# A state-space convolution mixed with linear attention: turn scratch and normaliser scratch laid out anew, index cast on VectorE, and a new issue list with new engine and ring choices

## The chip, the cores and the metric

The kernel runs on one core of one Trainium2 chip. The metric is the device time of one execution in microseconds. Before the change the median of three runs is 265.28 us (264.55 to 266.64). The engines are TensorE (PE, matmuls; PEld, its weight loads), VectorE (DVE), ScalarE (ACT), GpSimd (POOL) and SyncE (SP), which only issues transfers. A transfer is split over 16 DMA engines. DVE and ACT share the casts that bring matmul results from PSUM to SBUF.

## The reference

The input u has 2048 positions of 512 channels. Two results are mixed by a gate g of each position:

```python
x = A_u
g = _sigmoid((x * gate_w).sum(-1, keepdims=True))
a = _A_ref(x, ...)      # S4 convolution
b = _B_ref(x, ...)      # linear attention, 32 heads of 16
return g * a + (1 - g) * b
```

The convolution's kernel is K[d, l] = Re(sum over n of C * exp(dt*A*l) * dt*B), with 128 complex states for each channel; y is the causal convolution of u with K (in the reference by a transform of length 4096), plus u times Dskip. The attention forms q, k, v from one weight, maps q and k by a small weight of each head, takes the softmax of the result and of its negative as 32 features, and divides phi_q (phi_k^T v) by phi_q (sum of phi_k) for each head. A last weight wo follows.

## The kernel before

**Order of the work.** The kernel first makes a list of 1058 steps (class Plan, L71 on). A step has an engine, the steps it depends on, and the buffers it takes and drops. Then it emits them in the order of a string: each pair of characters of ORDER is a step's number. Every engine runs its own steps in that order and waits at a step whose inputs aren't there; so a late step holds up all that stands behind it on its engine. Three more strings hold choices: SIDES says for each step that may run on either of two engines which one it is (mostly casts on ACT or DVE, some copies on DVE or GpSimd, the output issues on SP or ACT); RINGS says which of two PSUM rings a step takes (psP, two tiles, or the one that exists at that stage); WARM adds idle matmuls to chosen steps, and is all zeros.

**Stages.** (1) Up to about 24 us: loads, sine tables TB, TI, TJ from an index, transposes of u (xps, L504), weight folds (wtp, wps), polar tables. (2) About 24 to 72 us: keys and values (pk L709, vp L757, kn L774) on PE, with the forward transform of u (psAu L591, psBu L616), whose result goes through the scratch XUd in DRAM. (3) From about 72 us: the tables C and D, then, for 16 units of 32 channels, the convolution kernel: tables A (A1 L1100, A2 L1105, A3 L1110) and R (Rh L1117, Rl L1121) on DVE, the product kps (L183) on PE, the transform of K in two stages (psA L190, psB L196), the product with the spectrum of u (t, L1231, L1234, on DVE), the inverse transform psz (L1263), the turn, and psy (L1341, L1354), which adds the attention's part and is multiplied with the gate by DVE (ou, L1363, L1366, L1369). In between come four query blocks (pq L843, zs L863, em L913, ops L932, and for the last block bpsL L946). Channels come in blocks: three of 128 (Q = 0, 1, 2), then 64, 32 and 32.

**The turn.** Between psz and psy the data must change from (t, x) on partitions to (x, r). For every block but the last this goes through a DRAM scratch Zd. psz's result is cast to Zr (two buffers; L149 by P.copy), written (step zw, L1276) and read back in two halves (step zr, L1285) into ZT:

```python
F.Zd = g.dram.tile([32, 4, 32, nd], BF16, ...)                        # t x r d
nc.sync.dma_start(out=F.Zd[:, :, r0:r0 + ns, :].rearrange("t x r d -> (t x) r d"), in_=box.Z[:])   # L1276
nc.sync.dma_start(out=F.Z[64 * th:64 * th + 64], in_=F.Zd[:, 2 * th:2 * th + 2].rearrange("t x r d -> (x r) t d"))   # L1285
```

nd is the block's channels and ns = 1024/nd, so a written run is always 2 KB on each of 128 partitions and a read run is nd x 2 bytes (256 B for nd = 128), 32 of them on each partition. A block of 128 has four writes of 256 KB and two reads of 512 KB. The last block (32 channels) has no scratch: its psz (pszn, L1297) gives the turned form directly, cast to Z by two steps Zn.

**The normaliser.** A query block's 1/denominator (times 1 - g) is made on ACT and DVE (z1 to z5, among them L880 and L886), written by SP to a scratch apd (step aw, L899) and read back to all partitions (step ar, L906), two steps of two reads of 256 KB, into ax. DVE then multiplies the exponentials Eq with it (em, emL, L913). The scratch has 8 rows of 2 KB for each read, and each row goes to 16 partitions:

```python
in_=g.apd[b, i].rearrange("h m c -> h (m c)").unsqueeze(1).to_broadcast([8, 16, 1024])   # L906
```

**Index cast.** Step ifc (L238) casts eight columns of index values from int32 to f32 with nc.scalar.copy; the identity (L239) and the other index columns (L246 to L254) on DVE wait for it, and behind them the arguments of the sines (tg1, L269).

**Loads and outputs.** All loads are issued by SP: parameters (L216), wqk (L1502), small weights (L1497 to L1499), u in four groups (L1492). XUX is read from XUd (L1184, L1186) ahead of each t. Outputs (out, L1380; outL, L995) are issued by SP or ACT, two transfers a step; an output step of a block stands behind the last ou (or bsg) of it.

Of the kernel before, what the change touches and what calls it, by code (L numbers as in the profile page):

```python
# [11 lines left out]
ALU = mybir.AluOpType  # L12
# [58 lines left out]
class Plan:  # L71

    DIGITS = "0123456789abcdefghijklmnopqrstuvwxyzABCDEFGHIJKLMNOPQRSTUVWXYZ-_"
    ORDER = ("040B0H0K0d0y0C0D0L0s0I070J0M0P0g000S110j0N08010z0T0m0Q0e2R0a0p0q0r0_0W2T100U0O0V14120Y2U2x0A2S050k130Z2y2V2X2Z0R190v0t0u"
             "0b0c0w2_0l0E0X2W1516172L1a061b2Y022-30311y33340n030f0-"
             "0h1e1f0i1w2J18321c0F0o2B2K2M1n1z1H1g1A1o2D2C1d1p1I091x1E1J351Q1R2F1B0x1C2E0G2H1q36372G2I2P382N2Q391F3b2O3c4C1S3a4J4L4K4M"
             "3d3e4Q4R3f4U1Y3g4N1r4O1h4V3h1L4Y4-"
             "4P3i4Z4_3j4W4S53542z57504T3k4X1Z515b5d58521s1D593l5c3n5i5e55565j3m5a1G3o5q5f5g5s5r5t3p3r3q1T5m5n5u3s5v5h5o5k5w5x5B1P4D4E"
             "3w2v5l5p4F5y5F5C3y1U5H3x5G5I5J5z5A1V5D5E3t3z5U3D5K5V5M5N3A3R3E2w3F5W5L1O5_3G5O5Q5X5Y5Z3B3C1W605R5S1N3K3M1K3S1M5-"
             "5P3L634G642A615T653N673T6869626a666m6n6o3U6p3V3W3X3Y6b6c6q6d6r6s1t3Z3H3-1X3_3O1i1j41401_4221431-"  # L80
             "1k1l204445466e272923222b282d4748243P491m2a4a2c2e4b4g2f4c2g4d252h2o4e4h4i4n1u4j3u3v2j4p2i2l2k2m2q2p6i262s4q4o1v4k2n4u2r2t"
             "6f4v4w6j4r3I2u4x4y4z6g4l8l3J4A8p8m6t6u6k6v8q3Q4f4s6x6h8k8o6l8n8r8s6y6z6w6A6C4m4t4B8C6G8t6I6K8w8x8y8u6B6H6J4H8D8v6L6M6N7d"
             "8z8A8E4I8B7e7f8I7g8F6F9e8Q8G8H9b6O6P8R7h7j7i6Q6R8J9f7M7N8S6S6T6U6Vaeaf7O8W8X8K7k9g8L8T8U8Z8-"
             "938M8N7l6D8_7m8V7n6W6X6Y8O8P8Y7P94an7o7pao7q6_70717r90917Qa47S9295ag7R6Z7s6-"
             "72aha8a9966Ea7akaca5ai73aa75979998ajap7677a69aalatamab74ad7TaBaC7t797u7v7U78au7y7z7V7w7x9caq9naras7AavaH7W9d9h9o9paw7X9v"
             "aY9waK7Y7ZaDaL9q9raZ7a9x9y9zaIc57B7-aM9kc69D9EaQaEbX9L7Cb_aF7D9M7_9Ac07EaRaG9iaxaz80ay9B818285bYaA7Ga-"
             "7IaJ86879j9Fc19s7Jb-"
             "9l9m9Na_7bc7aNaOaPc3cbb2b37HbZc283aS9C7FaT849G9H9I9t89aUaWaV8baX7cccc8c99O9u9P9Q9R888cb87Kb9b0c4caceb19J8abacfcgbg8dck9K"
             "8ecl8f8gbbbh8hbcbibob4cP9Sbpbqcd9T8ichci7L8jcBcCcjcsdYcYctcucycDczdZd-cQcR9Ucmd_cHcvcw9W9Xcnbj9VbwbkblbxcocIbre0eLcp9Ze1"
             "e2b5b6eMbse3eUeVcxb7bye4cqbtbu9Ybdbe9-"  # L90
             "9_cAcrcSbme5cZdOdScEbfcFcGcTcUe6a0a1bve7dTdRdWeNa2e8cJcKe9bzbAedeecLeRcNcOa3eSeaebeOcMc_ePbBd0ecd1d7cVd8d9cWeCdfcXeWdPdU"
             "d2daefege-e_eQd3dbdQdgeTdVd4dndodXdhdcg1g2dieDeEdjeXbKfAbCbnbDbEbFeYfBeZf0f1bGc-dpbLddg7dqbHd5f2drbMf3f4f5bNfGbIbJbOezdk"
             "eAfDdsfEeBeIf6f7feffdldtbPdebQdBfCfHehdueifFejdmf8fgeJd6ekdvfIfJdyf9fafhfbg4fifKg5g6dwfjdzfkfcdxdCdEfLdAdFfMg3g8dGg9dHfN"
             "fleFelfdfmfpdDdLgagbgcgddIeGemeKfqeHfOfPfQfRgeenepfneofreqeresgfggghgifSfTfUfofsbRgjbSgkdJftetglfVfYfZgmgngobUbVgqfufWdM"
             "dNbWgpf-fvfxfygreufwevewexbTeydKfzfXf_g0gvgwgsgtgugx")
# [103 lines left out]
def prepare(P, nc, g, evict, psum):  # L199
# [11 lines left out]
    def S(name, fn, r="", w="", deps=()):  # L211
        return P.add("ACT", name, fn, deps, rw=(r, w))
# [59 lines left out]
    def sine(out, v, kv, w, turn=False):  # L272
        S("tgs", lambda: act(out=out(), in_=(low(v()) if not turn else low(v()).rearrange("p (h t) -> p t h", h=2)), func=ACT.Sin, scale=TURN), r="act " + kv, w=w)
# [1352 lines left out]
```

## Time and profile before

| what | value |
|---|---|
| median of 3 runs | 265.28 us |
| profiled execution, its own time | 266.07 us |
| span of the profile (first to last instruction) | 264.3 us |
| mean granted TensorE clock | 0.932 |
| DVE, ACT, PE busy | 232.5, 221.5, 207.2 us |
| DMA traffic | 35.93 MB, mean 136 GB/s |
| ACT table loads | 11, 1.28 us each |

In the profile a row of groups reads: line, engine, operation, output<-input, partitions x elements, count | busy time, mean ns of one | idle time before them and its releaser. A row of the timeline begins with start and duration; in brackets stand the idle time of the engine before the row and what ended it. A name with q (SPq, ACTq) is an issue by the queue and not work of the engine. A row of waits reads: who <- whom, total us, times, longest. A row of stretches has for each engine busy us and (x instructions), and the last two numbers are the mean busy share of the 16 DMA engines (it can exceed 1, since packets of one engine overlap) and GB/s. A row of the DMA queues reads: packets, MB, share of 16 engines.

### The profile page before, as it was taken

The numbers are of one execution on the slowest core, as the hardware profiler recorded it, in microseconds if no ns is written. First come the engines' busy times: TensorE is split into PE (matmuls) and PEld (weight loads), VectorE is DVE, ScalarE is ACT, GpSimd is POOL, SyncE is SP. The second block draws the span as 40 slices with busy tenths as digits, with TensorE's granted clock in tenths as the row PEclk, the third lists the DMA queues.
The fourth block names the chain that finished last, engine by engine and source line by source line (L and its number), as shares of the span: only waits on it lengthen the run. The fifth ranks groups of instructions, "written<-read, shape, count | busy, mean of one in ns | idle before, by whom it ended". The sixth has DMA issues, their size and how long they took to land.

```text
span 264.3 us, 10050 instructions
## 1 busy us (share of the span) xinstructions
PE 207.2 (78%) x4491; PEld 143.7 (54%) x4512; DVE 232.5 (88%) x315; ACT 221.5 (84%) x305; POOL 8.2 (3%) x21
## 2 busy tenths in 40 slices
PE   0766999999864879889776768999997598999750
PEld 0655655656633533456555247665775176965540
DVE  6699989889799999999999997999997998997630
ACT  6999998998899999899999898999998597755100
POOL 4700000000000000000000000000000000000000
PEclk9999999999976599999998688999999799999985
DMA  6995000454501892204160655159554589999775
GB/s 201 189 219 171 0 4 2 122 145 138 154 8 36 245 266 97 82 20 153 56 195 9 208 195 167 42 162 180 142 172 147 172 203 234 188 189 162 156 110 96
DMA packets 63323, 35.93 MB, mean 136 GB/s; under 512 B 40496, under 2 KB 57776, under 8 KB 63280
## 3 DMA queue, kind: packets, MB, share of 16 engines
q1 hardware_dynamic: 61424, 34.76, 53.2%
q8 instruction: 35, 0.57, 1.0%
q10 hardware_dynamic: 1856, 0.52, 1.0%
q14 instruction: 8, 0.07, 0.1%
HBM read 22.17 MB, written 13.11 MB: 133 GB/s over the span
## 4 chain that ended last, share of the span: by engine, by line
DVE 35%; PE 34%; DMA 8%; issue 7%; ACT 7%; SPq 6%; DVEq 0%; ACTq 0%
PE pk L709 5%; PE vp L757 4%; DVE Eq L913 3%; DVE A L1105 3%; DVE A L1100 3%; DMA ZT<-Zd 3%; DVE R L1117 3%; DVE R L1121 3%; SPq L1492 3%; DMA ax<-apd 2%; PE kps L183 2%; DVE E L1053 2%; PE psz L1263 2%; PE kvp L774 2%; DMA apd<-apm 2%
## 5 line engine op out<-in xcount | busy, mean ns | idle before, releaser
L68 ACT ACTIVATE cs<-args 128x1024 bf16<-128x1024 f32 x32 | 30.7, 1067 | 0.7 <-PE args L1023 0.7
L183 PEld LDWEIGHTS <-A 128*32 128x32 bf16 x1536 | 26.5, 160 | 6.1 <-issue 2.3
L183 PE MATMUL kps<-R,A 128*32 128x64 bf16 x1536 | 28.2, 229 | 1.9 <-DVE R L1121 1.2
L1263 PE MATMUL psz<-t,TI 128*128 128x512 bf16 x51 | 17.4, 446 | 5.0 <-DVE t L1231 3.2
L1100 DVE TENSOR_TENSOR A<-Ctab,Dtab 128x2048 bf16<-128x2048 bf16 x16 | 19.5, 1216 | 1.6 <-PE kps L183 1.6
L149 ACT CAST Zr<-psz 128x1024 bf16<-128x1024 f32 x15 | 15.2, 1021 | 5.8 <-PE psz L1263 4.3
L1121 DVE TENSOR_TENSOR R<-E,cs 128x2048 bf16<-128x2048 bf16 x16 | 19.4, 1215 | 0.1
L1105 DVE TENSOR_TENSOR A<-Ctab,Dtab 128x2048 bf16<-128x2048 bf16 x16 | 19.4, 1216 | 0.0
L1117 DVE TENSOR_TENSOR R<-E,cs 128x2048 bf16<-128x2048 bf16 x16 | 19.4, 1215 | 0.0
L68 ACT ACTIVATE Ek<-pk 128x512 bf16<-128x512 f32 x32 | 16.7, 599 | 1.9 <-PE pk L709 1.7
L68 ACT ACTIVATE Eq<-pq 128x512 bf16<-128x512 f32 (+1 forms) x28 | 16.6, 685 | 0.8 <-PE pq L843 0.7
L1231 DVE TENSOR_TENSOR t<-XUX,XK 128x2048 bf16<-128x2048 bf16 x14 | 16.7, 1216 | 0.4 <-ACT XK L149 0.4
L68 ACT ACTIVATE E<-args 128x1024 bf16<-128x1024 f32 x16 | 16.4, 1035 | 0.5 <-DVE R L1121 0.5
L757 PE MATMUL vp<-WW,xT 128*128 128x512 bf16 x59 | 16.2, 406 | 0.7 <-issue 0.6
L149 ACT CAST XA<-psA 128x1024 bf16<-128x1024 f32 (+1 forms) x15 | 14.6, 1002 | 2.4 <-PE psA L190 2.4
L843 PE MATMUL pq<-xT,Wqp 128*128 128x512 bf16 x64 | 15.5, 380 | 0.3 <-ACT xT L149 0.3
L616 PE MATMUL psB<-XAu,TB 64*128 64x128 bf16 x256 | 11.6, 250 | 5.1 <-ACT xst L149 3.4
L149 ACT CAST XK<-psB 128x1024 bf16<-128x1024 f32 (+1 forms) x14 | 13.6, 989 | 2.2 <-DVE XK L151 1.3
L709 PE MATMUL pk<-WW,xT 128*128 128x512 bf16 x58 | 15.0, 380 | 0.4 <-issue 0.2
L616 PEld LDWEIGHTS <-TB 64*128 64x128 bf16 x256 | 9.6, 110 | 8.9 <-issue 8.8
L190 PE MATMUL psA<-W,KD 128*64 128x128 bf16 x256 | 10.0, 223 | 5.1 <-ACT cs L68 2.9
L65 ACT ACT_TABLE_LOAD x10 | 12.8, 1283 | 0.2
(211 smaller groups left out, 503.8 us busy)
## 6 DMA issues: line engine op xcount, KB each, us to landing
XUX<-XUd SPq DMA_DIRECT2D x32, 256.0 KB
XUd<-xst SPq DMA_DIRECT2D x8, 512.0 KB
ax<-apd SPq DMA_DIRECT2D x16, 256.0 KB
Zd<-Zr SPq DMA_DIRECT2D x15, 256.0 KB
ZT<-Zd SPq DMA_DIRECT2D x6, 512.0 KB
UD<-in_A_u_dram SPq DMA_DIRECT2D x16, 128.0 KB
XUd<-xst SPq DMA_DIRECT2D x8, 256.0 KB
wqk<-in_B_wqkv_dram SPq DMA_DIRECT2D x1, 1024.0 KB
```

What stands on the lines that cost most here:

```text
L68: return self.nc.scalar.activation(**kw)
L149: self.nc.scalar.copy(out=o, in_=i)
L183: nc.tensor.matmul(kps[32 * dj:32 * dj + 32, g4, e, :], lhsT=A[:, ka, :, :, d].rearrange("p a b -> p (a b)"), rhs=R[:, kr, d, :], start=(i ...
L616: nc.tensor.matmul(box.ps[:, c2, sl, :], lhsT=fc.TB[rows, b0:b0 + 2].rearrange("p a b -> p (a b)"), rhs=X.t[rows, k, r0 + sl].rearrange("p ...
L709: nc.tensor.matmul(box.ps[:], lhsT=xT[:, st, kt, :], rhs=g.WW[:, kt, :], start=(kt == 0), stop=(kt == 3))
L757: nc.tensor.matmul(box.ps[:], lhsT=xT[:, st, kt, :], rhs=g.WW[:, 4 + kt, :], start=(kt == 0), stop=(kt == 3))
L1100: nc.vector.tensor_tensor(out=c.A[:, 0:2].rearrange("p o a b c -> p (o a) b c"), in0=g.C[U // 8][:, 0:2, :, d0 % 256:d0 % 256 + 32].rearra ...
L1105: nc.vector.tensor_tensor(out=c.A[:, 2:4].rearrange("p o a b c -> p (o a) b c"), in0=g.C[U // 8][:, 1:3, :, d0 % 256:d0 % 256 + 32].rearra ...
L1117: nc.vector.tensor_tensor(out=c.R[:, :, :, 32:64], in0=t.E[:, 1].unsqueeze(1).to_broadcast([128, 2, 32, 32]), in1=t.cs[:], op=ALU.mult)
L1121: nc.vector.tensor_tensor(out=c.R[:, :, :, 0:32], in0=t.E[:, 0].unsqueeze(1).to_broadcast([128, 2, 32, 32]), in1=t.cs[:, ::-1, :, ::-1], o ...
L1231: nc.vector.tensor_tensor(out=box.t, in0=Ls[r0 // ns].X[:], in1=box.XK[:].unsqueeze(1).to_broadcast([128, 2, 1024]), op=ALU.mult)
L1263: nc.tensor.matmul(box.ps[:, hb, :], lhsT=fc.TI[:, k].rearrange("p t h a -> p (t h a)"), rhs=box.t[:, k, 512 * hb:512 * hb + 512], start=( ...
```

## The change

- The scratch Zd changes its axes from (t, x, r, d) to (r, x, t, d). The write has runs of nd x 2 bytes, and the read has one run of 32 x nd x 2 bytes for each partition (8 KB for nd = 128), in two transfers for each half, so four a block. The table TI is stored (h, a, t) instead of (t, h, a), so that psz's output partitions come as (x, t).
- The scratch apd holds every row twice (two writes of 64 KB), and a read takes 16 rows, each for 8 partitions.
- Step ifc runs on DVE.
- ORDER, SIDES and RINGS are new; WARM is "0". Decoded: 49 steps change their engine. Net of exchanges, DVE gets one more each of the casts XAu, XU, Y and bs3 and two more copies udc (UDp<-UD), and one fewer each of wTe (wT<-wtp) and wpe (WW, Wqp<-wps) and two fewer of XK; the selector product sel1 (selE, L458) goes from DVE to GpSimd, and of ten output steps five are on ACT instead of two. 39 takes change their PSUM ring. On SP the loads begin with wqk and the small weights. On PE the second stage of the last block (psB32) stands ahead of the second output group (bpsL) and not behind it, and the psy of the block of 64 stands behind pszn.

```diff
-    S("ifc", lambda: nc.scalar.copy(out=F.fi[:], in_=F.ii[:]), r="ic0", w="ic1")
+    V("ifc", lambda: nc.vector.tensor_copy(out=F.fi[:], in_=F.ii[:]), r="ic0", w="ic1")
...
-            nc.sync.dma_start(out=g.apd[b].rearrange("i h m c -> (i h m) c"), in_=Q.apm[:].rearrange("p s t -> p (s t)"))
+            for u in range(2):
+                nc.sync.dma_start(out=g.apd[b, :, :, u].rearrange("i h m c -> (i h) m c"), in_=Q.apm[:].rearrange("p s t -> p (s t)"))
...
-                                  in_=g.apd[b, i].rearrange("h m c -> h (m c)").unsqueeze(1).to_broadcast([8, 16, 1024]))
+                                  in_=g.apd[b, i].rearrange("h u m c -> (h u) (m c)").unsqueeze(1).to_broadcast([16, 8, 1024]))
...
-                        nc.tensor.matmul(box.ps[:, hb, :], lhsT=fc.TI[:, k].rearrange("p t h a -> p (t h a)"), rhs=box.t[:, k, 512 * hb:512 * hb + 512],
+                        nc.tensor.matmul(box.ps[:, hb, :], lhsT=fc.TI[:, k].rearrange("p h a t -> p (h a t)"), rhs=box.t[:, k, 512 * hb:512 * hb + 512],
...
-                nc.sync.dma_start(out=F.Zd[:, :, r0:r0 + ns, :].rearrange("t x r d -> (t x) r d"), in_=box.Z[:])
+                nc.sync.dma_start(out=F.Zd[r0:r0 + ns].rearrange("r x t d -> (x t) r d"), in_=box.Z[:])
...
-            nc.sync.dma_start(out=F.Z[64 * th:64 * th + 64], in_=F.Zd[:, 2 * th:2 * th + 2].rearrange("t x r d -> (x r) t d"))
+            for x in (2 * th, 2 * th + 1):
+                nc.sync.dma_start(out=F.Z[32 * x:32 * x + 32].rearrange("p t d -> p (t d)"), in_=F.Zd[:, x].rearrange("r t d -> r (t d)"))
...
-                                         rhs=fc.TI[:, k, :, :, x % 2].rearrange("p t h -> p h t"), start=(k == 0), stop=(k == 1), tile_position=(0, 32 * x),
+                                         rhs=fc.TI[:, k, :, x % 2, :], start=(k == 0), stop=(k == 1), tile_position=(0, 32 * x),
...
-        fc.TI = persist.tile([128, 2, 32, 2, 2], BF16, name="TI")
+        fc.TI = persist.tile([128, 2, 2, 2, 32], BF16, name="TI")
...
-        g.apd = dram.tile([4, 4, 8, 4, 256], BF16, name="apd")
+        g.apd = dram.tile([4, 4, 8, 2, 4, 256], BF16, name="apd")
```

The sine and scaling instructions that fill TI follow the new layout. Of ORDER, 1027 of the 1058 places differ; the strings are not shown, and what the prediction uses of them is said in words.

63 lines of the change are left out of this document (29 added, 34 removed).

## The prediction

> **What bounds the kernel now.** I read the page first, for the engines' totals, and then cut the span into four stretches.
>
> ```profile
> span 264.3 us, 10050 instructions
> PE 207.2 (78%) x4491; PEld 143.7 (54%) x4512; DVE 232.5 (88%) x315; ACT 221.5 (84%) x305; POOL 8.2 (3%) x21
> 0.00:24.00 24.00, 12.34 (x133) 10.87 (x134) 18.90 (x50) 21.46 (x28) 8.23 (x21) 1.00 0.99 214
> 24.00:72.00 48.00, 45.31 (x782) 28.81 (x789) 42.52 (x60) 43.46 (x82) 0.00 (x0) 1.00 0.28 77
> 72.00:240.00 168.00, 137.16 (x3118) 95.75 (x3130) 162.04 (x193) 152.47 (x190) 0.00 (x0) 0.92 0.54 143
> 240.00:264.30 24.30, 12.41 (x465) 8.26 (x462) 9.05 (x15) 4.11 (x7) 0.00 (x0) 0.82 0.73 124
> ```
>
> The columns of the last four rows are busy time of PE, weight loads, VectorE, ScalarE and GpSimd, then granted clock, DMA share, GB/s. VectorE idles 31.8 us in all. In 24 to 72 us TensorE is the fuller engine (45.3 of 48). From 72 to 240 us VectorE is the bound: 162.0 of 168, so 6.0 us of idle time is all that a better order can win there. The last 24.3 us are another stage: VectorE works 9.0 us of it and idles 15.3, so a chain of dependent steps and the output transfers set the end.
>
> Next the waits of VectorE, longest first, and the chain of waits around 200 us, because both reshaped transfers stand in it.
>
> ```profile
> DVE tgv L269 <- ACT TB L68: 2.2, 1, 2.2
> DVE xT L1366 <- PE psy L1341: 1.9, 2, 1.1
> DVE Eq L913 <- DMA ax<-apd: 1.7, 1, 1.7
> 193.80 4.54 DMA apd<-apm
> 200.34 5.88 DMA ax<-apd
> 212.47 7.92 DMA ZT<-Zd
> ```
>
> The chain spends 5.9 us on the normaliser's read and 7.9 us on the turn's read, but VectorE lost only 1.7 us to the first and 1.1 us (the larger of the two L1366 waits) to the second: the rest of both transfers lay beside other work. These smaller numbers are what shorter transfers can give directly.
>
> **The change part by part.** *Index cast on VectorE.* The rows of the first microseconds, ScalarE, VectorE and SP:
>
> ```profile
> 0.73 1.28 ACT L238 ACT_TABLE_LOAD   x1 [0.73 <-PEq L1610]
> 4.90 1.06 ACT L68 ACTIVATE TB<-tgv 128x1024 bf16<-128x1024 int16 x1 [1.38 <-DVE tgv L269]
> 2.26 0.93 DVE L239 TENSOR_SCALAR ident<-c,if 128x128 bf16<-128x128 f32 x1 [0.48 <-ACT if L238]
> 3.26 0.16 DVE L249 SCALAR_TENSOR_TENSOR one<-one 128x1 f32<-128x1 f32 x1
> 1.20 0.41 SPq L1502 DMA_DIRECT2D wqk<-in_B_wqkv_dram  x1
> ```
>
> The copy on ScalarE pulls in a table load of its own, 1.28 us, and that goes. But ScalarE idles 1.38 us before its first sine, waiting for VectorE, so what counts is VectorE's own 0.48 us wait for the copy, which becomes one small instruction there (0.16 us, an estimate from the column instruction of L249): 0.32 us. The new order also issues wqk first instead of behind one parameter, one issue of 0.41 us sooner. I take -0.4; bounds 0 (the inputs' transfers set this stretch, DMA share 0.99) and -1.28 (the whole load).
>
> *Normaliser read as 16 rows.* Three views: SP's issues, the transfer totals of 201 to 206 us, the wait on VectorE.
>
> ```profile
> 198.39 2.52 SPq L906 DMA_DIRECT2D ax<-apd  x4
> DMA packets 503, 0.97 MB, mean 195 GB/s; under 512 B 37, under 2 KB 37, under 8 KB 501
> q1 hardware_dynamic: 501, 0.95, 53.8%
> 205.10 1.22 DVE L913 TENSOR_TENSOR Eq<-Eq,ax 128x2048 bf16<-128x2048 bf16 x1 [1.71 <-DMA ax<-apd]
> ```
>
> A backlog of four reads is in flight, yet the 16 engines are busy 54% of the time: the read of 8 rows keeps about half of them at work. A packet of 2 KB takes 0.538 x 5 us x 16 / 501 = 86 ns, so a read of 128 packets takes 1.4 us on eight engines and 0.7 us on sixteen. VectorE waits for the first two reads: 1.4 us less. Against it the scratch is written twice, one more issue on SP ahead of the reads, four times in all; at the 0.41 us of the wqk issue above. Behind it on SP stand the reads themselves, which wait for its landing, and later XUX loads. So -1.0; bounds -1.7 (the whole wait) and +0.4 (the read was hidden, the extra issue is not). No row shows that 16 rows get 16 engines. The Trainium skill states it, DMA: Bandwidth & Descriptors, "Why a DMA increments its semaphore by 16 and not by 1": a copy uses the largest number of engines up to 16 that divides the slowest dimension of both sides, so 8 rows get 8 (the share of 54% agrees) and 16 get 16; by it the last of the four reads would land 2.75 us sooner.
>
> *Turn's scratch.* Zd is laid out so that the read takes rows of 8 KB (4 and 2 KB for the narrower blocks) and the write now goes out in pieces of 256 B (128, 64), where the write had 2 KB and the read the short pieces. The reads are four per block instead of two. Views: SP, VectorE, and transfer totals of 228.5 to 232.5 us (short reads) and 242.6 to 244.6 us (short output writes).
>
> ```profile
> 212.47 4.84 SPq L1285 DMA_DIRECT2D ZT<-Zd  x2
> 217.42 2.83 SPq L1186 DMA_DIRECT2D XUX<-XUd  x2
> 221.11 1.23 DVE L1366 TENSOR_TENSOR xT<-psy,gT 128x1024 bf16<-128x1024 f32 x1 [1.11 <-PE psy L1341]
> q1 hardware_dynamic: 2881, 0.73, 135.4%
> q1 hardware_dynamic: 996, 0.24, 68.7%
> ```
>
> A short read packet takes 1.354 x 4 x 16 / 2881 = 30 ns, so 4096 of them 7.7 us; the same megabyte at the 2 KB price is 512 x 86 / 16 = 2.75 us. A short write packet takes 0.687 x 2 x 16 / 996 = 22 ns. A write of one quarter therefore goes from 0.7 us to 1.4 to 1.9 us. From the last piece to the turned block: 8.4 us before, 4.2 to 4.7 after. SP's two reads no longer sit 4.84 us in the issue, and the XUX loads behind them are freed. What VectorE sees of all this is the 1.11 us; I take -1.1. Bounds: -1.9 (both L1366 waits) and +1.2 (reads hidden, the last write longer). Ten more issues on SP at about 0.6 us fall into its long waits. A rule of the Trainium skill speaks against this edit: the same page, "Specifications", says that transfers below 512 B are done by read-modify-write. The trace does not bear that out for writes: 22 ns against 30 ns for reads of the same length. By the rule a short write would cost double, and the gain of this edit would be about nothing.
>
> *The tail of the order.* I decoded both issue lists (each pair of characters is a step's number). In the old list the second-stage matmuls of the last block (psB32) stand behind the last output group (bpsL); in the new list they stand ahead of it. And the output steps are dealt out anew. TensorE, VectorE, SP, ScalarE's queue:
>
> ```profile
> 242.67 0.69 DVE L151 CAST XA<-psA 128x512 bf16<-128x512 f32 x1 [1.16 <-ACT XA L149]
> 243.42 1.02 PE L946 MATMUL bps<-wo,oT 128*128 128x512 bf16 x4 [0.44 <-DVE XA L151]
> 245.58 0.95 PE L196 MATMUL psB<-XA,TB 128*128 128x32 bf16 x32
> 257.00 0.69 DVE L1366 TENSOR_TENSOR xT<-psy,gT 128x512 bf16<-128x512 f32 x1 [0.74 <-PE psy L1341]
> 251.25 7.84 SPq L1380 DMA_DIRECT2D out_dram<-xT  x4
> 259.13 1.17 SPq L995 DMA_DIRECT2D out_dram<-xT  x2
> 260.40 1.27 SPq L1380 DMA_DIRECT2D out_dram<-xT  x2
> 252.54 6.84 ACTq L1380 DMA_DIRECT2D out_dram<-xT  x4
> ```
>
> psB32 had its data at 243.36 and began at 245.58: 2.2 us that the chain behind it (XK, t, psz, Z, psy, the last product, the last output) gets back. After the last product at 257.69 SP still worked off issues until 261.67. The new list leaves two issues on SP and two on ScalarE behind that product, 1.3 us, so up to 2.7 us; since ten issues still stand between the Z casts and them on SP, I take 1.0. ScalarE gets three more output steps, two issues each; two of these steps stand ahead of casts of the chain (XK, Z). At 0.4 us for an unhindered issue and 1.7 us for a mean one of that row they cost 0 to 3.3 us; I take 0.5, nearer the free ones, since ScalarE is idle for most of the tail. Together -2.7.
>
> *Engines of casts.* Counted from the decoded engine choices. Prices:
>
> ```profile
> L151 DVE CAST XAu<-psA 128x1024 bf16<-128x1024 f32 x8 | 9.5, 1216 | 1.5 <-PE psA L591 1.4
> L149 ACT CAST XAu<-psA 128x1024 bf16<-128x1024 f32 x8 | 8.2, 1032 | 0.0
> L151 DVE COPY UDp<-UD 128x1024 bf16<-128x1024 bf16 x5 | 2.0, 418 | 0.0
> L149 ACT COPY UDp<-UD 128x1024 bf16<-128x1024 bf16 x3 | 3.1, 1050 | 0.0
> L151 DVE COPY wT<-wtp 128x1024 bf16<-128x1024 bf16 x3 | 2.0, 679 | 0.0
> L481 POOL TENSOR_TENSOR diagD<-ident,Dcol 128x512 bf16<-128x512 bf16 x1 | 1.4, 1362 | 0.1
> ```
>
> Net on VectorE: one XAu and one XU cast more, one fold cast, two XK casts and the selector product (as long as a cast) fewer: -2 x 1.22; one Y and one bs3 more, at the 0.69 us of the 128x512 cast above, +1.4; two UDp copies +0.84; one wT copy -0.68; the index cast +0.16. Sum -0.7, and the part that falls after 72 us is -1.1. ScalarE: full casts net +1.03, wT +1.05, Y and bs3 about -1.3, UDp -2.1, index copy and table load -1.5, so -2.8, nearly all before 72 us. It is not the bound: taken as nothing, and -2.8 is the end of that range. The selector on GpSimd takes twice the 1.36 us of half its size, so about 2.7 us, behind an engine's work that is over by 24 us (8.23 us busy, none after). It is hidden by the 48 us of key work that come before the argument matmuls which read it; without that cover it would cost its 2.7 us. I take -0.7.
>
> *Order and rings elsewhere.* 39 PSUM takes change rings and nearly every step its place; WARM was all zeros and stays so; the TI layout changes no instruction count, and its matmuls read contiguous columns (0). No row prices a new order. Bounds: -3.2, what is left of the 6.0 us of idle time after the two waits above, and +5.5, the idle time that VectorE has in the 48 us before. I take +0.7: waits that go tend to be replaced in part.
>
> **Sum:** -0.4 - 1.0 - 1.1 - 0.7 - 2.7 + 0.7 = -5.2 us. The profiled execution took 266.07 us (span 264.3 and 1.8 around it), 0.8 above the median of 265.28. 266.07 - 5.2 = 260.9; against the median 260.1, which I forecast.
>
> **The rivals.** *More than that.* The new list makes use of short transfers, so that waits close that I left in: the order term at its end (-3.2 instead of +0.7) and the outputs at -2.7. That is -10.8, 254.5 us. For it: the tail's 15.3 us of idle time. Against: VectorE's 162 of 168 us leave little.
>
> *The waits only change owners.* Both transfers were hidden but for 2.8 us, and the tail is bound by output transfers (DMA share 0.73): only the start and the casts remain, -1.1, 264.2 us.
>
> *Slower: the short pieces hurt as writes.* The place is the pair of Zr buffers: psz can't refill one before its write has landed, and t, R and A on VectorE stand behind. A write is 0.7 to 1.2 us longer at the prices above. At 1.2 us each, five writes on VectorE's path cancel the 5.2 us, eight give +9.6 - 5.2 = +4.4, 269.7 us. By the rule of the Trainium skill, DMA: Bandwidth & Descriptors, "Specifications", the writes would double and three would do. For it: the DMA share of 1.35 at the short reads. Against: writes are spread, the reads were not.
>
> **How the numbers follow.** Forecast 0.50, more 0.14, owners 0.20, slower 0.16. A change within 1%, about what a measurement of this kernel can tell from none, is 262.6 to 267.9 us; so faster 0.64, same 0.20, slower 0.16. The range 254.5 to 268.0 leaves out half of the best case and two thirds of the worst, 0.18. Since it spans both signs, the forecast's own range is 257 to 262.6.
>
> **What would show it.** Right: no table load at L238; the four normaliser reads in flight with a DMA share near 1; SP's ZT issues at about 0.6 us each; no VectorE wait on ax or on psy L1341 near 200 to 221 us; VectorE's total down by about 0.7; psB32 directly behind its XA cast; the last issue within 2 us of the last product. Wrong: VectorE waits on psz or Zr with SP's Zd issues stretched (slower), or the idle time of 72 to 240 us above 8 us (the new order loses what the transfers won), or ScalarE's output issues standing ahead of the XK and Z casts for over a microsecond each.

## The result and the profile after

The changed kernel takes 268.18 us (median of 20 runs, 266.44 to 274.13) beside 264.83 us of the kernel before on the same chip (20 runs): ratio 1.0112, 95% interval 1.0077 to 1.0147. It is slower by about 3 us where I forecast 5 us less, and just outside the range. (Medians are of all runs; the ratio leaves disturbed executions out on both sides.)

The profiled execution of the changed kernel took 266.7 us, 0.6 us above that of before, so the two profiles differ by less than the runs do; its mean granted clock was 0.962, that of before 0.932. From its page, and from the table of stretches (busy time of PE, weight loads, VectorE, ScalarE, GpSimd; then clock, DMA share, GB/s):

```profile
span 264.9 us, 10098 instructions
PE 205.6 (78%) x4512; PEld 144.7 (55%) x4512; DVE 235.0 (89%) x317; ACT 219.2 (83%) x301; POOL 10.0 (4%) x22
0.00:24.00 24.00, 12.49 (x107) 11.70 (x107) 21.14 (x50) 16.52 (x21) 9.97 (x22) 1.00 1.03 208
72.00:240.00 168.00, 130.99 (x3040) 92.81 (x3038) 159.37 (x191) 154.87 (x194) 0.00 (x0) 0.96 0.55 146
```

Two things differ from before. VectorE works longer, 235.0 us instead of 232.5, and 2.2 us of that lie in the first 24. And in the stretch that it bounds, 72 to 240 us, it is busy for 159.4 of 168 us where it was busy for 162.0: its idle time there went from 6.0 to 8.6 us, although the clock in this stretch was higher (0.96 instead of 0.92). What it waits for in that stretch (total, times, longest):

```profile
DVE Eq L909 <- DMA ax<-apd: 3.6, 3, 1.8
DVE t L1230 <- ACT XK L144: 2.8, 1, 2.8
```

The wait for the normaliser, which shorter reads should have ended, went from 1.7 us to 3.6. SP's issues around the first two blocks, and VectorE's products on them, show how:

```profile
121.64 1.22 SPq L902 DMA_DIRECT2D ax<-apd  x2
122.91 0.59 SPq L1505 DMA_DIRECT2D wo<-in_B_wo_dram  x1
123.60 0.96 SPq L1180 DMA_DIRECT2D XUX<-XUd  x2
124.60 1.90 SPq L902 DMA_DIRECT2D ax<-apd  x2
126.17 1.23 DVE L909 TENSOR_TENSOR Eq<-Eq,ax 128x2048 bf16<-128x2048 bf16 x1 [0.53 <-DMA ax<-apd]
132.15 1.23 DVE L909 TENSOR_TENSOR Eq<-Eq,ax 128x2048 bf16<-128x2048 bf16 x1 [1.29 <-DMA ax<-apd]
209.83 1.23 DVE L909 TENSOR_TENSOR Eq<-Eq,ax 128x2048 bf16<-128x2048 bf16 x1 [1.81 <-DMA ax<-apd]
```

The new order splits a block's four reads: the second pair leaves behind a weight load and two loads of the transform, 1.7 us after the first pair's issue ended. The turn's reads are split in the same way, so the chain of waits still spends 7.90 us and 8.13 us on two of them; the issues themselves are short, 0.8 to 0.9 us for two:

```profile
191.28 7.90 DMA ZT<-Zd
232.03 8.13 DMA ZT<-Zd
188.02 0.80 SPq L1282 DMA_DIRECT2D ZT<-Zd  x2
189.69 1.01 SPq L1180 DMA_DIRECT2D XUX<-XUd  x2
190.75 0.94 SPq L1282 DMA_DIRECT2D ZT<-Zd  x2
```

### The profile page after: what moved, and what is told of

It reads as the page before. It is cut to its first block, busy times and chain, and to the rows that moved or that the text cites. A ratio compares the mean times of both kernels' runs of the same rounds, so it can differ in the third digit from the quotient of the medians.

```text
span 264.9 us, 10098 instructions
## 1 busy us (share of the span) xinstructions
PE 205.6 (78%) x4512; PEld 144.7 (55%) x4512; DVE 235.0 (89%) x317; ACT 219.2 (83%) x301; POOL 10.0 (4%) x22
## 4 chain that ended last, share of the span: by engine, by line
DVE 31%; ACT 23%; PE 18%; DMA 13%; SPq 7%; issue 6%; DVEq 0%; ACTq 0%
DMA ZT<-Zd 7%; ACT cs L68 5%; DVE t L1227 4%; DVE R L1117 4%; DVE A L1096 3%; PE kps L178 3%; DVE R L1113 3%; DVE A L1101 3%; PE psB L611 2%; ACT xst L144 2%; SPq L1489 2%; ACT L65 2%; SPq L354 2%; DVE xst L146 2%; PE pq L838 2%
## 5 line engine op out<-in xcount | busy, mean ns | idle before, releaser
L144 ACT CAST XK<-psB 128x1024 bf16<-128x1024 f32 (+1 forms) x16 | 16.0, 1020 | 7.9 <-PE psB L191 4.7
L1259 PE MATMUL psz<-t,TI 128*128 128x512 bf16 x60 | 15.5, 380 | 3.3 <-DVE t L1227 1.5
L752 PE MATMUL vp<-WW,xT 128*128 128x512 bf16 x64 | 17.3, 398 | 0.0
L144 ACT CAST XA<-psA 128x1024 bf16<-128x1024 f32 x15 | 15.0, 1044 | 1.6 <-PE psA L185 1.6
L191 PE MATMUL psB<-XA,TB 128*128 128x128 bf16 (+2 forms) x192 | 10.2, 200 | 5.8 <-ACT E L68 2.4
```

The lines of the kernel that those rows point to most:

```text
L144: self.nc.scalar.copy(out=o, in_=i)
L752: nc.tensor.matmul(box.ps[:], lhsT=xT[:, st, kt, :], rhs=g.WW[:, 4 + kt, :], start=(kt == 0), stop=(kt == 3))
```

## The experiments

Each was timed in five rounds beside the kernel before. Line numbers differ by up to five between kernels, since the strings have different lengths. I name steps as the prediction did: kps is a product of the mixing kernel, psB, psz and psy are products of the transform, zw and zr the writes and reads of its scratch.

**The layouts alone, and the strings alone.**

```diff
 changed kernel (e1_layouts)
-    ORDER, SIDES, RINGS as changed; ifc on VectorE
+    ORDER, SIDES, RINGS as before; ifc on ScalarE
 kernel before (e2_strings)
-    ORDER, SIDES, RINGS as before
+    ORDER, SIDES, RINGS as changed
```

> The kernel before with the two scratch layouts (turn and normaliser) alone; old issue list, engines and rings, index cast on ScalarE. Theory 1 (the new strings lose, the layouts give what was forecast): 1 to 2.5 us faster than before, ratio 0.990 to 0.996, VectorE waits on ax and psy near 200 to 221 us smaller. Theory 2 (the short pieces hurt as writes): 3 to 8 us slower, ratio 1.011 to 1.03, with longer landings of the Zd writes and VectorE waiting behind psz.

> The kernel before with the new ORDER, SIDES and RINGS alone; old layouts, index cast on ScalarE. Theory 1: 4 to 6 us slower than before, ratio 1.015 to 1.023, with the first pk about 1 us late and the tail's psy waiting longer for ZT than in the changed kernel. Theory 2: 2 to 5 us faster, ratio 0.98 to 0.993.

Layouts alone: 0.9961 (0.9916 to 1.0006). Strings alone: 1.0288 (1.0173 to 1.0404). The loss is in the strings (order, engines and rings), and they are worse still without the short transfers that they were made for. This is the row of stretches and VectorE's longest wait for the layouts alone:

```profile
72.00:240.00 168.00, 136.04 (x3152) 95.87 (x3163) 165.42 (x198) 154.81 (x196) 0.00 (x0) 0.97 0.56 147
DVE t L1235 <- DMA XUX<-XUd: 1.0, 1, 1.0
```

With the old order and the new layouts VectorE is busy for 165.4 of the 168 us, and no wait for ax or psy is left. That is 3.4 us more than before, what I had expected of these two parts, but most of it goes with the clock and not with them: the clock of this row is 0.97, that of before 0.92. The stretch of 110 to 210 us shows it. The rows are of four kernels with before's order: before, both layouts with the selector on GpSimd (a later experiment), the normaliser's layout alone (another), and both layouts alone.

```profile
110.00:210.00 100.00, 82.01 (x1979) 58.00 (x1984) 96.49 (x104) 93.35 (x121) 0.00 (x0) 0.94 0.46 130
110.00:210.00 100.00, 82.50 (x1984) 57.92 (x1988) 97.29 (x105) 94.19 (x122) 0.00 (x0) 0.95 0.50 131
110.00:210.00 100.00, 81.65 (x2120) 59.42 (x2124) 99.83 (x108) 97.20 (x126) 0.00 (x0) 1.00 0.53 141
110.00:210.00 100.00, 82.30 (x2138) 59.65 (x2138) 99.80 (x108) 96.83 (x127) 0.00 (x0) 1.00 0.51 137
```

At a clock of 0.94 to 0.95 VectorE idles 3.5 us without the layouts and 2.7 with both; at 1.00 it idles 0.2 us, with the old turn as with the new (1.4 and 1.6 in two more profiles of this order at that clock). So the layouts can be credited with some 0.8 us there at most, in line with the 1.0 us of the timed runs, whose interval reaches no gain at all.

**Order or engines?** The two can be parted only roughly, since the rings go with the order.

```diff
 changed kernel (e5_order_rings_back)
-    ORDER, RINGS as changed
+    ORDER, RINGS as before
 changed kernel (e6_sides_back)
-    SIDES as changed
+    SIDES as before
```

> The changed kernel with the order of before and the PSUM rings of before; layouts, engines of the casts and the index cast stay as changed. Theory 'order': the new order puts the normaliser's product and the narrow blocks' copies ahead of transfers that have not landed, so with the old order back the time falls to that of the layouts alone, 264 to 265 us (ratio 0.995 to 1.000 to before), and VectorE no longer waits for ax. Rival 'engines': the new engines of the casts are what costs (VectorE busy +2.5 us), then the time stays at 267 to 269 us (1.008 or more).

> The changed kernel with the engines of the casts of before; order, rings, layouts and the index cast stay as changed. Theory 'order': no gain to speak of, 267 to 270 us (ratio 1.007 to 1.018), the VectorE waits for ax are still there. Rival 'engines': 263.5 to 265.5 us (0.995 to 1.001).

1.0523 (1.0452 to 1.0593) and 1.0611 (1.0543 to 1.0679). Both halves are far slower than either whole, so neither theory had it: an order is made for the engines that it was made with, and this test says nothing on the price of either.

**Where in time?** So I kept order, engines and rings together and changed them by stretches. First the part ahead of the first kps and the rest; then the rest cut at the thirteenth kps; then the middle cut at the eighth. In the profile of before these three stand at 107.5, 211.3 and 163.4 us (the row below is the first), and the traces of the mixed kernels change over at about 110, 210 and 165 us; the 72, 198 and 160 us of the expectations are too early.

```profile
107.50 1.22 PE L183 MATMUL kps<-R,A 128*32 128x64 bf16 x64 [1.25 <-DVE R L1121]
```

The index cast is on VectorE in the first two kernels, on ScalarE in the others.

```diff
 new layouts; ORDER, SIDES, RINGS of each step
 e7_front_back     -as changed  +as before up to kps#0, as changed behind
 e8_front_only     -as changed  +as changed up to kps#0, as before behind
 e10_middle_only   -as changed  +as changed from kps#0 to kps#12, else as before
 e11_tail_only     -as changed  +as before up to kps#12, as changed behind
 e17_mid_first     -as changed  +as changed from kps#0 to kps#7, else as before
```

> The changed kernel, in which all that before issues ahead of its first product of the mixing kernel (about 72 us) keeps before's order, engines and rings; the rest is as changed. If the loss is the front's 2.5 us (selector product on GpSimd, W product stretched), 264 to 265.5 us (ratio below 1.002). If the loss is made behind 72 us, 267 to 269 us, as the run with the selector back on VectorE (1.016) speaks for; the waits for ax at 120 to 210 us are still there.

> The other half: order, engines and rings of the changed kernel up to about 72 us, those of before behind it, with the new layouts. If the loss is made behind 72 us, 264 to 265.5 us (ratio 0.995 to 1.002) although the front is 2 us late. If it is the front's, 267 to 268 us (1.007 to 1.012).

> New layouts with the order, engines and rings of before, except from the first to the thirteenth product of the mixing kernel (about 72 to 198 us), where those of the changed kernel stand; index cast on ScalarE. If the loss behind the front is the middle's (waits for ax, blocks in another order) 266.5 to 268 us, 1.004 to 1.010 of before. If it is the tail's, as the layouts alone: 263.5 to 265 us, 0.993 to 0.999.

> The complement: order, engines and rings of before up to about 198 us, those of the changed kernel behind it; new layouts, index cast on ScalarE. If the loss is the tail's: 266.5 to 268.5 us (1.004 to 1.012). If my term for the tail (2.7 us gained) was right, it stands alone here: 261 to 262.5 us (0.985 to 0.990).

> As the run with the changed middle (1.010 of before), but the changed order, engines and rings stand only from the first to the eighth product of the mixing kernel, about 72 to 160 us; before's stand ahead and behind. If the cost is made there (normaliser's products and table passes up to 8 us early, the transform's copies late): 267 to 269 us, 1.006 to 1.013. If it is made by the order between 160 and 198 us, where VectorE's waits in that run begin behind 190 us: 263.5 to 265.5 us, 0.993 to 1.001.

| strings as changed in | ratio to before | 95% | VectorE idle in 110 to 210 us, at clock |
|---|---|---|---|
| nothing (layouts alone) | 0.9961 | 0.9916 to 1.0006 | 0.2, 1.00 |
| first to eighth kps | 1.0048 | 1.0011 to 1.0085 | 2.0, 1.00 |
| first to thirteenth kps (middle) | 1.0102 | 1.0066 to 1.0137 | 2.9, 1.00 |
| behind the thirteenth kps (tail) | 0.9984 | 0.9939 to 1.0030 | 1.6, 1.00 |
| up to the first kps (front) | 1.0066 | 1.0028 to 1.0105 | 3.7, 0.95 |
| behind the first kps | 1.0065 | 1.0027 to 1.0103 | 4.5, 0.98 |
| everything | 1.0112 | 1.0077 to 1.0147 | 5.1, 1.00 |

Against the layouts alone the middle costs 1.4%, the front 1.0%, the tail 0.2% (the last within the intervals). The first half of the middle costs 0.9%, between my two forecasts for it. The front is the least sure: its timed runs had a mean clock of 0.932, those of the layouts alone 0.947. The parts add up to more than the whole, 2.7% beside 1.5%, but that difference is no larger than its uncertainty; that a part which is late hides the next part's waits would explain it and is not shown. So neither "front" nor "behind" was right alone, and the tail, on which I had put half of the gain, has neither that gain nor the loss that was the other forecast. The stretch rows of the changed middle alone (72 to 240 us, then 110 to 210), the row of the changed kernel for 110 to 210 us, and two of the waits of VectorE in the changed middle:

```profile
72.00:240.00 168.00, 133.91 (x3125) 94.61 (x3139) 161.19 (x192) 153.41 (x191) 0.00 (x0) 0.96 0.55 144
110.00:210.00 100.00, 79.41 (x1983) 56.87 (x1988) 97.14 (x105) 95.34 (x124) 0.00 (x0) 1.00 0.53 141
110.00:210.00 100.00, 80.13 (x2133) 57.98 (x2131) 94.93 (x104) 96.32 (x127) 0.00 (x0) 1.00 0.53 144
DVE t L1227 <- ACT XK L144: 1.8, 2, 0.9
DVE zs L881 <- ACT den L68: 0.7, 1, 0.7
```

In 72 to 240 us VectorE loses 4.2 us against the layouts alone, at nearly the same clock (0.96 and 0.97), in many waits of under a microsecond, for ScalarE's casts, for products and for transfers. No single one stands out. In 110 to 210 us, at a clock of 1.00 in all of them, its idle time is 0.2 to 1.6 us in five profiles of the old order, 2.9 with the changed middle and 5.1 in the changed kernel: here most of the loss of the middle is seen directly.

**The waits for ax, and SP's order in the middle.** Two candidates for a single cause. The first leaves the normalising out (the products multiply the features by themselves), so that nothing waits for the reads; the second puts only SP's transfers of the middle back.

```diff
 changed kernel (e14_no_ax)
-                nc.vector.tensor_tensor(out=e, in0=e, in1=Q.ax[:, 2 * ip:2 * ip + 2], op=ALU.mult)
+                nc.vector.tensor_tensor(out=e, in0=e, in1=e, op=ALU.mult)
 changed middle alone (e16_mid_sp_back)
-    SP's steps between kps#0 and kps#12 in the changed order
+    the same steps in the order of before
```

> The changed kernel with the normaliser's product multiplying the features by themselves, not by the broadcast normaliser (left out: the normalising; the transfers run on as before). VectorE no longer waits for ax, 3.6 us in the profile of the changed kernel. If those waits are what the new order costs: 264 to 265.5 us, 0.996 to 1.001 of before. If VectorE only waits elsewhere then (the next wait takes it over): 267 to 268.5 us, 1.007 to 1.012.

> The run with the changed middle (72 to 198 us) was 1.010 of before. Here the transfers that SP issues in that stretch go back to before's order; the order on the engines stays as changed. Theory 'the queue': reads placed badly on SP are what delays, the time comes down to 264 to 266 us (0.996 to 1.002). Rival 'the engines' order': the normaliser's products come up to 8 us earlier and the copies of the transform up to 8 us later than before, and that is what leaves VectorE idle behind 190 us; the time stays at 267 to 269 us (1.007 to 1.014).

Without the waits for ax: 1.0083 (1.0037 to 1.0128), so they are worth at most part of the loss. Other waits took over; VectorE is busy for 161.4 us of 72 to 240 instead of 159.4, and now stands 1.5 us before an A step:

```profile
DVE A L1096 <- PE kps L178: 2.1, 3, 1.5
```

With SP's order of before: 1.0188 (1.0134 to 1.0241), slower than the changed middle as it was, and above both forecasts. SP's changed order belongs to the engines' changed order; put back, one read of the normaliser comes 4.5 us late:

```profile
DVE Eq L909 <- DMA ax<-apd: 4.5, 1, 4.5
```

So SP's order cannot be put back alone, and the test does not part it from the order on the engines. Which exchange of steps in the middle costs most stays open.

**The front's single steps.**

```diff
 kernel before (e3_ifc)
-    S("ifc", lambda: nc.scalar.copy(out=F.fi[:], in_=F.ii[:]), r="ic0", w="ic1")
+    V("ifc", lambda: nc.vector.tensor_copy(out=F.fi[:], in_=F.ii[:]), r="ic0", w="ic1")
 changed kernel (e4_sel_dve)
-    SIDES: sel1 on GpSimd
+    SIDES: sel1 on VectorE
 layouts alone (e12_sel_pool)
-    SIDES: sel1 on VectorE
+    SIDES: sel1 on GpSimd
```

> The kernel before with the index cast on VectorE alone. The prediction's price: 0.3 us faster. The changed kernel's trace (cast 1.32 us on VectorE beside the 2.0 us iota on GpSimd, identity 0.9 us later) says: nothing or up to 0.5 us slower, ratio 0.998 to 1.003.

> The changed kernel with the selector product back on VectorE. If GpSimd's 1.9 us product stretches the VectorE instructions beside it (W 2.14 against 0.46 us), and this delays the dense stretch of TensorE: 0.5 to 1.5 us faster than the changed kernel, ratio to before 1.005 to 1.010. Rival (the selector's 1.2 us on VectorE cancels it, or the start is covered): as the changed kernel, 1.011.

> New layouts with all of before's order, engines and rings, and only the selector product on GpSimd instead of VectorE. Theory 'VectorE's instructions are stretched beside GpSimd's': a VectorE instruction beside the 1.9 us product is 1 to 2 us longer in the profile and the time is 0.3 to 1.5 us above that of the layouts alone (0.998 to 1.002). Rival 'it is hidden work': VectorE loses 1.2 us of work and the time is that of the layouts alone or less (0.990 to 0.997).

The index cast alone: 0.9988 (0.9936 to 1.0041), no difference. The selector back on VectorE in the changed kernel: 1.0159 (1.0065 to 1.0253), not faster; the selector on GpSimd with the layouts alone: 1.0022 (0.9989 to 1.0054), 0.6% above them, though the two intervals overlap. Taking 1.2 us of work off VectorE gains nothing that can be measured in either place. Beside the selector the other VectorE instructions were only some tenths longer here, not the 1 to 2 us that I expected. In the changed kernel they were; its first microseconds on GpSimd and VectorE:

```profile
1.11 2.00 POOL L41 IOTA tgc<- 128x2048 f32 x1
11.23 1.90 POOL L453 TENSOR_TENSOR selE<-m,b 128x1024 bf16<-128x1024 bf16 x1
1.81 1.32 DVE L233 CAST if<-ii 128x8 f32<-128x8 int32 x1
3.17 0.29 DVE L234 TENSOR_SCALAR ident<-c,if 128x128 bf16<-128x128 f32 x1
11.27 2.14 DVE L276 TENSOR_TENSOR W<-w,one 128x256 bf16<-128x256 bf16 x1
```

The cast of 8 columns ends at 3.13 us, when GpSimd's iota ends (3.11). W ends at 13.41, behind the selector product (13.13); before it took 0.46 us, beside GpSimd instructions of 0.2 to 0.5 us:

```profile
10.40 0.46 DVE L281 TENSOR_TENSOR W<-w,one 128x256 bf16<-128x256 bf16 x1
```

The iota stood in the way before as well: the identity, which came first then, lasted from 2.26 to 3.19 us (0.93 us), and takes 0.29 us now that it runs behind the iota. It ends at 3.46 us, 0.27 later than before.

**SP's order in the tail.** In the changed kernel the last write of the scratch stands behind the reads of the block before it, and the last reads leave at 253.69 us. The three PE rows ahead of the last are an output group, psB32 and the second half of the last block's psz:

```profile
244.49 2.32 SPq L1282 DMA_DIRECT2D ZT<-Zd  x4
246.85 0.42 SPq L1272 DMA_DIRECT2D Zd<-Zr  x1
253.69 3.05 SPq L1282 DMA_DIRECT2D ZT<-Zd  x4
256.85 5.17 SPq L1377 DMA_DIRECT2D out_dram<-xT  x8
252.22 0.59 ACT L144 CAST Z<-psz 128x512 bf16<-128x512 f32 x1 [3.04 <-DMA out_dram<-xT]
243.47 1.04 PE L942 MATMUL bps<-wo,oT 128*128 128x512 bf16 x4
245.64 0.95 PE L191 MATMUL psB<-XA,TB 128*128 128x32 bf16 x32
251.01 1.16 PE L1294 MATMUL psz<-TI,t 128*32 128x64 bf16 x64 [1.10 <-DVE Z L146]
252.63 0.64 PE L1338 MATMUL psy<-ZT,TJ 64*32 64x64 bf16 x59
```

```diff
 changed kernel, order of the steps (e9_zw_first)
 Zr#14
+zw#14
 psB32#1
...
 zr#6
...
 zr#7
...
-zw#14
```

> The changed kernel with one move: on SP the last short write to the scratch (the narrow block's, whose cast ends at 244.21 us) goes ahead of the four reads of the block before it, so that it need not wait until 246.85 us. Theory 'the tail loses on SP's order': the last block's reads leave some 2.4 us earlier and the time falls by 1.5 to 2.5 us, to 0.993 of the changed kernel, 1.002 to 1.006 of before. Rival 'the tail follows the short pieces' landing': the write lands at the same 252 us because the pieces are what takes 5 us, and the time stays at 1.009 to 1.013.

1.0114 (1.0069 to 1.0159): nothing gained. In the profile of this kernel the write leaves right behind its cast, at 246.68 us, in a run that is some 2.4 us later at that point than the changed kernel's. It takes 5.5 us to land (252.17), as the rival said, and even then the last reads could not leave: they wait until 255.90 us, when the 64-column block's psy (252.63 us above, 255.14 here) has given back their one buffer. That psy stands behind both halves of psz in the new order, ahead of both in the old (246.90 and 249.47 us in the profile of before).

**Where the layouts' gain went.** One row of SP's waits and three rows of the end, with the layouts alone:

```profile
SPq L1287 <- DMA out_dram<-xT: 4.0, 1, 4.0
247.33 5.56 SPq L1287 DMA_DIRECT2D ZT<-Zd  x4
249.01 9.87 ACTq L1382 DMA_DIRECT2D out_dram<-xT  x4
256.71 0.69 DVE L1368 TENSOR_TENSOR xT<-psy,gT 128x512 bf16<-128x512 f32 x1 [3.77 <-PE psy L1343]
```

A read of the scratch waits 4.0 us for an output, though the two share no data. The trace shows eight semaphores for the transfers of this stretch, given out over both queues. The turn's reads are four instead of two, and the third has the semaphore of an output that ScalarE had issued at 249.01 us: that output landed at 252.09 us, and the read left at 252.11. The first edit takes that output to SP, behind the reads; the second also takes one of SP's last outputs to ScalarE. A third kernel has the normaliser's layout without the turn's.

```diff
 layouts alone (e13_out_on_sp)
-    SIDES: out#1 on ScalarE
+    SIDES: out#1 on SP
 the same (e18_outs_split)
-    SIDES: out#1 on ScalarE, out#6 on SP
+    SIDES: out#1 on SP, out#6 on ScalarE
 kernel before (e15_norm_alone)
-            nc.sync.dma_start(out=g.apd[b].rearrange("i h m c -> (i h m) c"), in_=Q.apm[:].rearrange("p s t -> p (s t)"))
+            for u in range(2):
+                nc.sync.dma_start(out=g.apd[b, :, :, u].rearrange("i h m c -> (i h) m c"), in_=Q.apm[:].rearrange("p s t -> p (s t)"))
...
-                                  in_=g.apd[b, i].rearrange("h m c -> h (m c)").unsqueeze(1).to_broadcast([8, 16, 1024]))
+                                  in_=g.apd[b, i].rearrange("h u m c -> (h u) (m c)").unsqueeze(1).to_broadcast([16, 8, 1024]))
```

> The run with the new layouts alone was 3 us ahead of before at 245 us and lost it: the narrow block's second pair of reads issued at 252.11 us, 3.98 us after the first pair, on a semaphore whose holder, an output that ScalarE issued at 249.01 us, landed at 252.09 us. Here that output's two transfers go from ScalarE to SP, behind the four reads; nothing else is changed. Theory 'the turn's split reads ran into a semaphore still held': the pair issues within 1 us of the first, the time falls by 2 to 4 us to 261 to 262.5 us, 0.982 to 0.990 of before. Rival 'the narrow block's write in 64-byte pieces is what is late': unchanged, 263.5 to 265 us (0.993 to 0.999).

> The run with the output behind the reads on SP, and in addition the last of SP's narrow outputs (two transfers) on ScalarE. In that run the last product's copy ended at 253.84 us, 3.6 us earlier than with the layouts alone, but SP's eight output issues lasted to 258.75 us, the last pair behind a semaphore that ScalarE's output held. If SP's issues are what ends last, the last issue ends by 256.6 us and the time is 1 to 2.5 us below that run's: 262 to 263.5 us, 0.985 to 0.991 of before. If the landing of the outputs is the limit whoever issues them: 0.992 to 0.997.

> Before with the normaliser in 16 rows alone (one write more per block, reads of 16 rows). My term: 1.0 us gained, 264 to 265 us (0.994 to 0.998). If the layouts' gain is all the turn's: 1.000 within 0.003.

0.9939 (0.9893 to 0.9984), 0.9954 (0.9914 to 0.9993) and 0.9993 (0.9951 to 1.0034). With the output on SP:

```profile
247.95 2.81 SPq L1287 DMA_DIRECT2D ZT<-Zd  x4
250.80 4.51 SPq L1382 DMA_DIRECT2D out_dram<-xT  x6
255.36 1.22 SPq L996 DMA_DIRECT2D out_dram<-xT  x2
257.50 1.25 SPq L1382 DMA_DIRECT2D out_dram<-xT  x2
253.15 0.69 DVE L1368 TENSOR_TENSOR xT<-psy,gT 128x512 bf16<-128x512 f32 x1 [0.74 <-PE psy L1343]
```

The four reads leave together (2.81 us instead of 5.56) and the last copy is 3.6 us earlier, as the semaphore theory says. But the time fell by 0.2% only, 0.6 us and not 2 to 4, and that within the intervals: SP now issues ten output transfers behind the reads, until 258.75 us, where it issued eight until 259.26. Dealing them out again brought nothing that can be measured; its last issue on SP ended at 257.75 us, and its time is in the range that I gave for the landing of the outputs as the limit. So the semaphore's wait is shown, and what it costs in the end is not. Both versions are faster than before by about half a per cent, and than the changed kernel by 1.6 to 1.7%.

How much the turn itself gained is read from its transfers: size of each and the median time from issue to landing, first with the normaliser's layout alone (old turn), then with both layouts.

```profile
Zd<-Zr SPq DMA_DIRECT2D x15, 256.0 KB, 3.6
ZT<-Zd SPq DMA_DIRECT2D x6, 512.0 KB, 8.2
Zd<-Zr SPq DMA_DIRECT2D x15, 256.0 KB, 4.2
ZT<-Zd SPq DMA_DIRECT2D x12, 256.0 KB, 6.0
```

For the third block, from the issue of the last write to the landing of the last read, it is 11.8 us with the old turn (218.98 to 230.76) and 10.4 with the new (220.10 to 230.46).

## Why the prediction was wrong

The step that failed is "No row prices a new order ... I take +0.7", together with the tail of 2.7 us gained. By the ratios the order, engines and rings cost 1.5% against the layouts alone (1.0112 less 0.9961), 4.0 us, or 2.5 to 5.5 by the intervals, where my terms for the start, the engines, the tail and the order made -3.1. What the runs show in its place is idle time of VectorE: in 110 to 210 us, at the same clock of 1.00, 0.2 to 1.6 us with the old order, 2.9 with the changed middle and 5.1 in the changed kernel. The layouts gave 1.0 us (0.9961) where I had 2.1. Point by point:

- *Start, -0.4.* Wrong. The table load went and ScalarE is relieved (16.5 us busy in 24, not 21.5), but the cast took 1.32 us, not 0.16, and the identity ends 0.27 us later, where I had taken 0.32 off. I had priced the cast by a VectorE instruction that ran after the iota. The Trainium skill, SBUF — State Buffer, section "Who interferes with whom", says that VectorE in its two-port modes, which casts can enter, and GpSimd share one pair of ports, and that whoever comes second waits out the other's whole instruction. The row agrees: the cast ends 0.02 us behind the iota. Alone it cost nothing that can be measured (0.9988).
- *Normaliser, -1.0.* The transfer did what I priced: from the issue of the first of four reads to the landing of the last it took 9.4 us before (198.39 to 207.79) and 6.8 with this layout alone (196.68 to 203.45), close to the 2.75 us that I had expected. In time it is worth 0.2 us alone, and from 1.3 gained to 0.9 lost is possible. The old order had only 1.7 us of waits on it, at a low clock; the new order made 3.6 of them, and it splits the reads.
- *Turn, -1.1.* Right in kind, too large in size. From the last piece to the turned block I had 8.4 us become 4.2 to 4.7; measured, 11.8 became 10.4. I had priced 8 KB pieces by the byte at the 2 KB price, 2.75 us for a megabyte, but with the layouts alone a packet of 8 KB takes 574 ns in the mean, not four times 86: 128 of them are 4.6 us on 16 engines. And I had priced every write in pieces of 256 B; the narrow block's write, in pieces of 64 B, lands 5.0 us after its issue, where it took 2.4 before. What the semaphore takes from this gain is not shown; with it out of the way both layouts give 1.6 us (0.9939), within the intervals of the 1.0. The turn was not run alone.
- *Engines, -0.7 on VectorE.* It was +2.5: the cast 1.3 and W 1.7 longer beside GpSimd, with a table pass (1.50 us) 0.7 and the turn's matrices 0.6 longer as well, and the identity 0.6 shorter. The count of casts was not the error; that GpSimd's work lengthens VectorE's instructions beside it was put at nothing. That this costs time in the end is not shown: with the selector back on VectorE the kernel is not faster.
- *Tail, -2.7.* Measured +0.6 (0.9984 less 0.9961) for all that lies behind the thirteenth kps, with 1.7 to either side. psB32 did move ahead of the second output group, but the first group, which had run at 239.00 and 240.09 us, now runs at 243.47 and 244.56, right ahead of it. So psB32 starts at 245.64 us where it had started at 245.58, and the 2.2 us were not there to win; its second XA cast also ends 1.5 us later (244.87). psy of the block before fell behind both halves of psz. ScalarE's Z cast, whose row names its output issue, did not wait for that: the issue was over at 251.24 us and the second half of psz at 252.17, 0.05 us before the cast. The outputs did get shorter, from 4.0 to 2.4 us between the end of the last copy and the last issue, but the last copy starts at 258.98 us, not 257.00. My list of waits had also left out the longest of before, 2.9 us of VectorE for the last psy (L1369) in this stretch.
- *Order elsewhere, +0.7.* The middle alone costs 3.7 us (1.0102 less 0.9961), within my bounds (-3.2 to +5.5) but far from the value that I took. I had named idle time above 8 us between 72 and 240 us as the sign of being wrong; it is 8.6. The 6.0 us of before, from which I had worked out what could be won, went in good part with the low clock of that profile: with both layouts and the old order VectorE idles 2.7 us in 110 to 210 us at a clock of 0.95, and 0.2 to 1.6 at 1.00.

The rival on the slow side had another mechanism, short writes holding up the pair of Zr buffers. It did not happen: VectorE has no wait on psz or Zr in the profile of the changed kernel, and the layouts with those writes are not slower than before. The strings alone, with writes of 2 KB runs, are slower still (1.0288). The rule that I set against them, read-modify-write below 512 B in the Trainium skill, DMA: Bandwidth & Descriptors, section "Specifications", comes without a price; that a write doubles was my own step. No doubling shows: of the packets of 256 B half are the turn's, its reads before and its writes after, and they take 25.8 ns in the mean before and 21.5 in the changed kernel. But the pieces are not free: with them the 15 writes land in a median of 4.2 us instead of 3.6.

Shown by runs are: the loss is in the strings, most of it between the first and the thirteenth kps, and there it is idle time of VectorE; no loss of the tail can be measured. Not shown are which exchange in the middle costs most, how much of the front's cost is its lower clock, and what the semaphore costs.

## What to carry to other kernels

An order written out by hand is one object with its engines and rings: the old order with the new engines, or the new order with the old ones, was 5 to 6% slower than before, while the two wholes lie 1.1% apart. Price it by one number, the idle time of the bounding engine in its stretch, and compare that number at the same granted clock only: with both layouts and the old order it was 2.7 us in 110 to 210 us at a clock of 0.95, and 0.2 to 1.6 at 1.00. Doubt every gain that the old order leaves less room for than the term claims. When a transfer is split in two, look in the waits for a read that waits for an output: here that was a semaphore, not data. And before counting on a step that moves ahead of another, look what moves into the place that it leaves.

## What the runs showed that I had not expected

- VectorE beside GpSimd: a cast of 128x8 took 1.32 us and a product of 128x256 took 2.14 us, each until GpSimd's instruction was over. With the selector back on VectorE the product still took 0.94 us, until GpSimd's next instruction, a 0.95 us memset, was over (12.22 and 12.17 us). With the selector on GpSimd in the old order, nothing like it happened: the W product was over before the selector began.
- The granted clock, which lies between 0.91 and 0.96 in the timed runs of most of these kernels, is worth about as much as the whole change. A straight line through the executions that the ratios use, one slope for all kernels, falls by 0.6 us for each 0.01 of it, but it explains only about a fifth of their scatter. At 0.94 it gives 264.9 to 265.5 us for before, by batch, 267.9 for the changed kernel, 268.0 for the changed middle, 267.8 for all behind the first kps, 266.5 for the changed front, 265.8 for the changed tail and 264.4 for the layouts alone, with 0.3 to 1.0 us to either side of each. So the cost of the middle does not come from the clock; the front's falls from 2.8 to 2.1 us against the layouts alone.
